# A gelu layer's forward and backward pass: a fixed order, shared half matmuls, and transposes by DMA

## The chip, the cores and the metric

The kernel runs on one core of one Trainium2 chip. A core has a matrix engine (TensorE, PE in the profile; its weight loads are PEld), a vector engine (VectorE, DVE), a scalar engine for activation functions (ScalarE, ACT), a general engine (GpSimd, POOL) and a queue engine (SyncE, SP). Operands lie in SBUF (128 partitions), matmul results in eight PSUM banks of 512 floats per partition; DMA moves data between DRAM and SBUF, within SBUF too, and can transpose 2-byte data on the way. Every engine takes its instructions in a fixed order and waits on semaphores for what other engines produce. DMAs are issued from the queues of SP, ACT and POOL.

The metric is device time of one execution in microseconds (us).

## The reference, cut to what matters

```python
B, S, D, F = 1, 2048, 448, 1792          # bf16 throughout

def fwd(x, w1, b1, w2, b2):
    h = einsum("bsd,df->bsf", x, w1) + b1
    h = gelu(h, approximate=True)         # tanh form
    return einsum("bsf,fd->bsd", h, w2) + b2

out, vjp = jax.vjp(fwd, x, w1, b1, w2, b2)
return (out, *vjp(grad_out))              # out, gx, gw1, gb1, gw2, gb2
```

So there are six large products: u = x w1, out = gelu(u + b1) w2, q = grad_out w2^T, gh = q times gelu'(u + b1), gx = gh w1^T, gw1 = x^T gh, gw2 = h^T grad_out, and the column sums gb1 and gb2. D = 448 is 3 x 128 + 64: each product over D has three full steps of 128 rows and a left-over of 64.

## The kernel before, in words

**Tiling.** F is 14 tiles of 128 ("ft"), S is 4 blocks of 512 rows ("b"), and a block is 7 pairs of ft tiles ("c"). Everything in the forward part is held transposed, F or D on the partitions: `xT_q` and `gT_q` hold a block of x and of grad_out, `w1_sb` holds w1, `w2T_sb` holds w2 transposed and halved.

**Forward part, per pair.** For each of the two ft tiles, four matmuls of 512 columns make u in a PSUM bank (L242). The fourth covers columns 320 to 447 of x; the part that the third has already counted is zeroed in the weights, and one of its rows carries b1, with a row of ones in `xT_q`. ACT reads the bank twice (gelu into `hT_blk`, L244; a square, L245), DVE reads it twice with float results (L246, L247). Then, for both tiles together (1024 elements per partition), ACT does a tanh (L248) and a square (L249), and DVE two operations (L250, L251) that give gelu' less one in `Ep`. Four more matmuls make q (L261; the overlap is zeroed in `gT_q`), and DVE multiplies `Ep + 1` by q, straight from PSUM, into `ghT_blk` (L263). POOL stores the pair's `hT_blk` and `ghT_blk` to DRAM.

**Output products.** While block b is worked on, the out and gx of block b-1 are made: per 128 rows, 14 matmuls of 448 columns (emit_M2, L191; emit_M6, L204), evicted by DVE with b2 added (L193) or by ACT (L206). SP stores them.

**Start.** Eight matmuls on zeros, then x and grad_out of block 0 and all of w2 are transposed on PE against an identity matrix that POOL makes (L100, L102, L171, L172), and copied out of PSUM by DVE and ACT. x and grad_out of blocks 1 to 3, and w1 as `w1T_sb`, are transposed by DMA from SP (L87 to L92, L272).

**Weight gradients.** These need h and gh with S on the partitions. Both are transposed by DMA from their DRAM copies: 14 transposes of 512 KB for h (L316), 14 for gh (L340). gw2 is 14 groups of 16 matmuls of 448 columns (L319); gw1 is made by column ranges of 256, 512, 512 and 512 (L377), its left-over 64 rows as half-width matmuls, two of them side by side on the two column halves of the array (L383). DVE adds up gb1 and gb2 (L311, L355 to L358), POOL reduces across partitions (L323, L363).

**Order.** Instructions are written in program order, and a scheduler places them on each engine at compile time by readiness and its own costs, so that PE's order differs from the source. Some edges are pinned by hand: transposes in a chain, plain DMAs after a batch of transposes (`pdma`), the stores of the last part after the last transpose.

Of the kernel before, what the change touches and what calls it, by code (L numbers as in the profile page):

```python
# [19 lines left out]
def kernel(  # L20
# [19 lines left out]
    assert B == 1  # L40
    NS = S // P
    NF = F // P
    KD = (D + P - 1) // P
    DL = D - (KD - 1) * P
    DOV = D - P
    assert DL == 64 and D % 16 == 0 and NF % 2 == 0
# [4 lines left out]
    SYNC_DEP = mybir.DependencyInfo(mybir.DependencyClass.Sync, mybir.DependencyReason.DATA)  # L51
    ORDER_DEP = mybir.DependencyInfo(mybir.DependencyClass.NoSync, mybir.DependencyReason.SCHED_ONLY)
# [8 lines left out]
    psum1 = ctx.enter_context(tc.tile_pool(name="psum1", bufs=3, space=bass.MemoryType.PSUM))  # L61
    psum4 = ctx.enter_context(tc.tile_pool(name="psum4", bufs=2, space=bass.MemoryType.PSUM))
    psum_acc = ctx.enter_context(tc.tile_pool(name="psum_acc", bufs=3, space=bass.MemoryType.PSUM))
    io = ctx.enter_context(tc.tile_pool(name="io", bufs=1))
    qpool = ctx.enter_context(tc.tile_pool(name="qpool", bufs=2))

    hT_dram = dram.tile([F, S], BF16, name="hT_dram")
    ghT_dram = dram.tile([F, S], BF16, name="ghT_dram")
    hT_dram_v = hT_dram.rearrange("(ft p) s -> p ft s", p=P)
    ghT_dram_v = ghT_dram.rearrange("(ft p) s -> p ft s", p=P)  # L70

    ident = const.tile([P, P], BF16, name="ident")
    make_identity(nc, ident[:])

    def chain(insts, first_after):
        prev_name = first_after
        for k, i in enumerate(insts):
            if prev_name is not None:
                tc.add_manual_dep(i.ins, prev_name, SYNC_DEP if (k == 0) else ORDER_DEP, reason="DMA transpose batch ordering")
            prev_name = i.ins.name  # L80
        return insts[-1]

    def load_quarter(q):
        rows = slice(q * SB, (q + 1) * SB)
        xq = qpool.tile([P, KD, SB], BF16, name="xT_q")
        ts = []
        ts.append(nc.sync.dma_start_transpose(out=xq[:, 0:KD - 1, :], in_=x2[rows, 0:(KD - 1) * P]))  # L87
        ts.append(nc.sync.dma_start_transpose(out=xq[:, KD - 1, :], in_=x2[rows, DOV:D]))
        nc.gpsimd.memset(xq[0:1, KD - 1, :], 1.0)
        gq = qpool.tile([P, KD, SB], BF16, name="gT_q")  # L90
        ts.append(nc.sync.dma_start_transpose(out=gq[:, 0:KD - 1, :], in_=g2[rows, 0:(KD - 1) * P]))
        ts.append(nc.sync.dma_start_transpose(out=gq[:, KD - 1, :], in_=g2[rows, DOV:D]))  # L92
        nc.gpsimd.memset(gq[0:DL, KD - 1, :], 0.0)
        return xq, gq, ts

    def pe_transpose_rows(dst, src_rows, j, on_act=False):
        ps = psum_acc.tile([P, KD, P], BF16, name="ps_acc")
        t_first = None
        for kt in range(KD - 1):
            ti = nc.tensor.transpose(ps[:, kt, :], src_rows[:, kt * P:(kt + 1) * P], ident[:])  # L100
            t_first = t_first or ti
        nc.tensor.transpose(ps[:, KD - 1, :], src_rows[:, DOV:D], ident[:])  # L102
        if on_act:
            ev_i = nc.scalar.copy(out=dst[:, :, j * P:(j + 1) * P], in_=ps[:])
        else:
            ev_i = nc.vector.tensor_copy(out=dst[:, :, j * P:(j + 1) * P], in_=ps[:])  # L106
        return t_first, ev_i

    fb = ExitStack()
    tmp = fb.enter_context(tc.tile_pool(name="tmp", bufs=3))  # L110
    blk = fb.enter_context(tc.tile_pool(name="blk", bufs=2))

    w2T_sb = const.tile([P, KD, F], BF16, name="w2T_sb")
    nc.vector.memset(w2T_sb[:, 0, 0:SB], 0.0)
    pw = psum1.tile([P, SB], F32, name="ps1")
    for i in range(8):
        nc.tensor.matmul(pw[:], lhsT=w2T_sb[:, 0, 0:P], rhs=w2T_sb[:, 0, 0:SB], start=True, stop=True)

    x_nat0 = tmp.tile([P, SPB, D], BF16, name="x_nat0", bufs=1)
    grp1 = [nc.sync.dma_start(out=x_nat0[:], in_=x2[0:SB, :].rearrange("(j p) d -> p j d", p=P))]  # L120
    w1_sb = const.tile([P, KD, F], BF16, name="w1_sb")
    nc.gpsimd.memset(w1_sb[0:DL, KD - 1, :], 0.0)

    def load_w1_cols(f0, f1, engs):
        fsl = slice(f0, f1)
        res = []
        for kt in range(KD - 1):
            res.append(engs[kt % len(engs)].dma_start(out=w1_sb[:, kt, fsl], in_=w1[kt * P:(kt + 1) * P, fsl]))
        res.append(engs[(KD - 1) % len(engs)].dma_start(out=w1_sb[DL:P, KD - 1, fsl], in_=w1[(KD - 1) * P:D, fsl]))
        return res  # L130

    def after(insts, prev_group):
        for i in insts:
            for pi_ in prev_group:
                tc.add_manual_dep(i.ins, pi_.ins.name, SYNC_DEP, reason="stagger startup loads")
        return insts

    grp1 += load_w1_cols(0, 512, [nc.scalar, nc.sync])
    grp1.append(nc.scalar.dma_start(out=w1_sb[0:1, KD - 1, :], in_=b1.rearrange("(o f) -> o f", o=1)))
    g_nat0 = tmp.tile([P, SPB, D], BF16, name="g_nat0", bufs=1)  # L140
    grp2 = [nc.sync.dma_start(out=g_nat0[:], in_=g2[0:SB, :].rearrange("(j p) d -> p j d", p=P))]
    w2_sb = const.tile([P, NF, D], BF16, name="w2_sb")
    grp1.append(nc.gpsimd.dma_start(out=w2_sb[:, 0:2, :], in_=w2[0:2 * P, :].rearrange("(ft p) d -> p ft d", p=P)))
    grp2.append(nc.gpsimd.dma_start(out=w2_sb[:, 2:NF // 2, :], in_=w2[2 * P:F // 2, :].rearrange("(ft p) d -> p ft d", p=P)))
    grp2 += load_w1_cols(512, 1024, [nc.sync, nc.gpsimd])
    after(grp2, [grp1[0], grp1[3]])
    grp3 = load_w1_cols(1024, F, [nc.gpsimd, nc.sync])
    grp3.append(nc.gpsimd.dma_start(out=w2_sb[:, NF // 2:NF, :], in_=w2[F // 2:F, :].rearrange("(ft p) d -> p ft d", p=P)))
    b2_bc = const.tile([P, D], BF16, name="b2_bc")
    grp3.append(nc.gpsimd.dma_start(out=b2_bc[:], in_=b2.rearrange("(o d) -> o d", o=1).to_broadcast((P, D))))  # L150
    after(grp3, [grp2[0], grp2[1]])

    xq0 = qpool.tile([P, KD, SB], BF16, name="xT_q")
    for j in range(SPB):
        pe_transpose_rows(xq0, x_nat0[:, j, :], j)
    nc.vector.memset(xq0[0:1, KD - 1, :], 1.0)
    gq0 = qpool.tile([P, KD, SB], BF16, name="gT_q")
    quarters = {0: (xq0, gq0)}

    def emit_gq0(pe_after, act_after):  # L160
        for j in range(SPB):
            t_first, ev_i = pe_transpose_rows(gq0, g_nat0[:, j, :], j, on_act=True)
            if j == 0:
# [21 lines left out]
    def emit_M2(b, j, hT_blk):  # L185
        if ("o", b) not in out_stage:
            out_stage[("o", b)] = io.tile([P, SPB, D], BF16, name="o_blk")
# [247 lines left out]
```

## Time and profile before

| | us |
|---|---|
| median of the 2 timed runs | 301.2 (301.1, 301.3) |
| span of the profiled execution, first to last instruction | 301.8 |
| start, until the first gh tile is done | 24.5 |
| forward part, until gw2 begins | 24.5 to 206.9 |
| gw2 and gw1 matmuls | 206.9 to 297.3 |
| end, after the last matmul | 4.5 |
| busy: PE, DVE, ACT, POOL | 284.4, 209.8, 147.6, 71.5 |

The profiled execution is not one of the timed runs; nothing of it was measured besides the span, which lies 0.6 above their median. In the page, a group line reads: line of the kernel, engine, operation, output and inputs with shapes, count, then busy time and mean duration in ns, then the idle time of the engine just before these instructions and what ended it. The chain is read as start, length, what; it goes back from the last instruction through whatever released each step. Matmuls are pipelined and their ends modelled, so the length of one (379 ns for 512 columns) is more than the distance between two.

### The profile page before, as it was taken

To read this page: it belongs to the slowest core of one execution; us is meant where nothing else is said; L and a number is where in the kernel's file an instruction comes from. 1 tells how busy PE (TensorE), PEld (TensorE's weight loads), DVE (VectorE), ACT (ScalarE), POOL (GpSimd) and SP (SyncE) were. 2 spreads that over 40 slices of the span, in tenths; PEclk is the share of its full clock that TensorE was granted. 3 is DMA by queue.
4 is the path that set the end of the run, shared out by engine and by line. 5 is a ranking of instruction groups with operands and counts; after the bars stand their busy time and mean duration, and the time that the engine had idled before them with its cause. 6 is when DMAs were issued, how large, how long until landed. Compare 5 with 4: busy or idle time off the path is not lost.

```text
span 301.8 us, 4020 instructions
## 1 busy us (share of the span) xinstructions
PE 284.4 (94%) x1520; PEld 142.5 (47%) x1520; DVE 209.8 (70%) x317; ACT 147.6 (49%) x236; POOL 71.5 (24%) x89
## 2 busy tenths in 40 slices
PE   4589799999999999999999999999999999799994
PEld 1355344444444444444444444555555558245542
DVE  0258999999999999878999778605600027857760
ACT  1099987759695756677665576112121212021211
POOL 2451010821063200522212111000210001242252
PEclk9999999999999999999999999999999999799998
DMA  4673197720579945743212314095889899999861
GB/s 134 192 206 137 41 182 168 303 114 37 130 189 375 389 155 103 213 165 130 104 72 92 116 42 187 15 223 78 169 178 171 181 213 195 183 222 164 283 206 61
DMA packets 96761, 49.18 MB, mean 163 GB/s; under 512 B 78803, under 2 KB 92596, under 8 KB 96742
## 3 DMA queue, kind: packets, MB, share of 16 engines
q1 hardware_dynamic: 91188, 31.60, 46.9%
q0 software_dynamic: 5264, 17.06, 15.0%
q10 hardware_dynamic: 290, 0.27, 0.4%
q8 instruction: 12, 0.20, 0.3%
q14 instruction: 7, 0.06, 0.1%
HBM read 7.92 MB, written 21.57 MB: 98 GB/s over the span
## 4 chain that ended last, share of the span: by engine, by line
PE 43%; DVE 9%; SPq 5%; ACT 4%; DMA 2%; issue 1%; POOL 0%; POOLq 0%; DVEq 0%
PE ps_acc L191 6%; PE ps_acc L204 6%; SPq L340 4%; DVE Ep L250 2%; DVE ghT_blk L263 2%; DVE Bt L246 2%; DMA gh_nat<-ghT_dram 2%; PE ps_2370 L377 2%; ACT Bt L249 2%; ACT Ct L248 1%; DVE Ep L251 1%; PE ps_2487 L377 1%; PE ps_2605 L377 1%; PE ps_2641 L377 1%; PE ps_2623 L377 1%
## 5 line engine op out<-in xcount | busy, mean ns | idle before, releaser
L191 PE MATMUL ps_acc<-w_sb,hT_blk 128*128 128x448 bf16 x224 | 47.7, 353 | 0.2
L204 PE MATMUL ps_acc<-w1T_sb,ghT_blk 128*128 128x448 bf16 x224 | 45.6, 353 | 0.0
L250 DVE SCALAR_TENSOR_TENSOR Ep<-Bt,A 128x1024 bf16<-128x1024 f32 x28 | 34.3, 1224 | 12.0 <-ACT Bt L249 11.7
L248 ACT ACTIVATE Ct<-Bt 128x1024 bf16<-128x1024 f32 x28 | 30.2, 1079 | 25.3 <-DVE Bt L246 25.3
L261 PEld LDWEIGHTS <-w2T_sb 128*128 128x128 bf16 x224 | 21.8, 98 | 27.5 <-issue 3.4
L242 PEld LDWEIGHTS <-w_sb 128*128 128x128 bf16 x224 | 22.1, 99 | 25.2 <-issue 2.8
L215 POOL DMA_DIRECT2D ghT_dram<-ghT_blk x28 | 20.3, 726 | 56.4 <-DVE ghT_blk L263 56.3
L355 DVE TENSOR_TENSOR gb_acc<-gh_nat 128x512 f32<-128x512 bf16 x7 | 4.8, 692 | 39.9 <-DMA gh_nat<-ghT_dram 33.1
L191 PEld LDWEIGHTS <-hT_blk 128*128 128x128 bf16 x224 | 21.8, 98 | 22.6 <-ACT hT_blk L244 0.9
L204 PEld LDWEIGHTS <-ghT_blk 128*128 128x128 bf16 x224 | 21.9, 98 | 21.2
L319 PEld LDWEIGHTS <-h_blk 128*128 128x128 bf16 x224 | 21.9, 98 | 20.5
L215 POOL DMA_DIRECT2D hT_dram<-hT_blk x28 | 20.3, 727 | 45.7 <-ACT hT_blk L244 31.3
L249 ACT ACTIVATE Bt<-Ct 128x1024 f32<-128x1024 bf16 x28 | 30.1, 1075 | 0.3
L377 PEld LDWEIGHTS <-x_all 128*128 128x128 bf16 x192 | 19.0, 100 | 21.1 <-issue 5.0
L357 DVE TENSOR_TENSOR gb_acc<-gb_acc,gh_nat 128x512 f32<-128x512 f32 x42 | 28.6, 723 | 0.3
L363 POOL PARTITION_ALL_REDUCE gb_all<-gb_acc x7 | 14.8, 2108 | 58.9 <-DVE gb_acc L358 58.9
L251 DVE TENSOR_TENSOR Ep<-Ct,Ep 128x1024 bf16<-128x1024 bf16 x28 | 19.2, 687 | 0.3
L206 ACT CAST gx_blk<-ps_acc 128x448 bf16<-128x448 f32 x16 | 8.4, 527 | 20.1 <-PE ps_acc L204 20.1
L193 DVE TENSOR_TENSOR o_blk<-ps_acc,b_bc 128x448 bf16<-128x448 f32 x16 | 9.8, 620 | 3.8 <-PE ps_acc L191 3.8
L311 DVE TENSOR_TENSOR gsum<-gsum,g_all 128x448 f32<-128x448 f32 x14 | 8.7, 625 | 0.5
L177 ACT ACTIVATE w2T_sb<-ps_acc 128x512 bf16<-128x512 bf16 x14 | 8.5, 730 | 0.0
L106 DVE COPY xT_q<-ps_acc 128x512 bf16<-128x512 bf16 x4 | 1.7, 425 | 9.7 <-PE ps_acc L102 9.7
(492 smaller groups left out, 468.7 us busy)
## 6 DMA issues: line engine op xcount, KB each, us to landing
hT_dram<-hT_blk POOLq DMA_DIRECT2D x28, 256.0 KB, 3.0
ghT_dram<-ghT_blk POOLq DMA_DIRECT2D x28, 256.0 KB, 2.7
out_dram<-o_blk SPq DMA_DIRECT2D x4, 448.0 KB
x_all<-in_x_dram SPq DMA_DIRECT2D x1, 1792.0 KB, 14.5
g_all<-in_grad_out_dram SPq DMA_DIRECT2D x1, 1792.0 KB
out_dram<-gx_blk SPq DMA_DIRECT2D x4, 448.0 KB, 3.1
out_dram<-gw_all SPq DMA_DIRECT2D x2, 784.0 KB, 5.5
out_dram<-gw_all SPq DMA_DIRECT2D x3, 384.0 KB, 2.7
```

Of the source, the lines that this page charges most:

```text
L191: nc.tensor.matmul(ps_o[:, 0:D], lhsT=hT_blk[:, ft, j * P:(j + 1) * P], rhs=w2_sb[:, ft, :], start=(ft == 0), stop=(ft == NF - 1))
L204: nc.tensor.matmul(ps_x[:, 0:D], lhsT=ghT_blk[:, ft, j * P:(j + 1) * P], rhs=w1T_sb[:, ft, :], start=(ft == 0), stop=(ft == NF - 1))
L215: i = eng.dma_start(out=out, in_=in_)
L242: mm_i = nc.tensor.matmul(ps1[:], lhsT=w1_sb[:, kt, fcols], rhs=xq[:, kt, :], start=(kt == 0), stop=(kt == KD - 1))
L248: tanh_i = nc.scalar.activation(out=Ct[:], in_=Bt[:], func=ACT.Tanh, scale=1.0 / 3.0)
L249: nc.scalar.activation(out=Bt[:], in_=Ct[:], func=ACT.Square)
L250: nc.vector.scalar_tensor_tensor(out=Ep[:], in0=Bt[:], scalar=1.0, in1=A[:], op0=ALU.subtract, op1=ALU.mult)
L251: nc.vector.tensor_tensor(out=Ep[:], in0=Ct[:], in1=Ep[:], op=ALU.subtract)
L261: nc.tensor.matmul(ps4[:], lhsT=w2T_sb[:, kt, fcols], rhs=gq[:, kt, :], start=(kt == 0), stop=(kt == KD - 1))
L319: nc.tensor.matmul(ps_w[:, 0:D], lhsT=h_blk[:, st, :], rhs=g_all[:, st, :], start=(st == 0), stop=(st == NS - 1))
L357: nc.vector.tensor_tensor(out=acc[:], in0=acc[:], in1=gh_nat[:, 2 * k:2 * k + 2, :], op=ALU.add)
L377: nc.tensor.matmul(ps_w[:, 0:wpair], lhsT=x_all[:, st, kt * P:(kt + 1) * P], rhs=gh_pair[:, st, :], start=(st == 0), stop=(st == NS - 1))
```

## The change

The forward part is written anew, in a fixed order on every engine (no scheduler), in 28 steps i, one per pair, over all blocks.

- **Two steps ahead.** Step i makes u and h of pair f = i + 2 (`LEAD = 2`, starting at i = -2) and q and gh of pair i.
- **Left-over halves side by side.** The 64 left-over rows of u sit in partitions 64 to 127 (`wt1`), those of q in partitions 0 to 63 (`w2T_t`). Each is a matmul over 64 rows, and the two are issued in turn, to the two row halves of the array and to different PSUM banks. b1 is no longer a row of the product: it is turned to a column on PE once and added by ACT.
- **Elementwise work.** ACT writes u + b1 as bf16 into SBUF (`U`), and gelu, the square and tanh work from there on 1024 elements; DVE uses bf16 operations with one input and an immediate, or with two inputs, and only the product with q still reads PSUM.
- **Transposes.** x and grad_out of block 0 and all of w2 come by DMA transpose. gh goes from SBUF to SBUF by DMA transpose (`turn_gh`, three per block) into `gh_nat` and is not stored to DRAM; h still goes through DRAM.
- **Output products** are filled in after each step: up to 4 pairs of matmuls in steps before 14, up to 8 from then on, the rest after step 27. At most four outputs are open at a time; each is stored by POOL as soon as it is evicted.
- **Weight gradients.** gw1 comes first, then gw2; ACT evicts each group and issues its store itself. The sums for gb1 and gb2 are interleaved on DVE.
- PSUM has two pools of four banks: u, q and gw2 share one; the outputs and gw1 the other.

The core of the diff (removed lines of the old forward part are left out):

```diff
+    sched = ctx.enter_context(tc.manual_schedule())
...
+    def pe_tails(f, k):
+        if k is not None:
+            PQ[k] = [psq.tile([P, SB], F32, name="pq", tag="pq") for _ in range(2)]
+        for a in range(2):
+            if f is not None:
...
+                nc.tensor.matmul(PU[f][a][:], lhsT=wt1[DL:P, fc], rhs=xT[b][DL:P, KF, :], start=False, stop=True,
+                                 tile_position=(DL, 0), skip_group_check=True)
+            if k is not None:
...
+                nc.tensor.matmul(PQ[k][a][:], lhsT=w2T_t[0:DL, fc], rhs=gT[b][0:DL, KF, :], start=True, stop=False,
+                                 tile_position=(0, 0), skip_group_check=True)
...
+    def act_forward(f):
...
+            nc.scalar.activation(out=U[f][:, a, :], in_=PU[f][a][:], func=ACT.Identity, bias=b1T[:, ft:ft + 1])
+        nc.scalar.activation(out=hT[b][:, 2 * p:2 * p + 2, :], in_=U[f][:], func=ACT.Gelu_apprx_tanh)
+        nc.gpsimd.dma_start(out=hT_dram_v[:, 2 * p:2 * p + 2, b * SB:(b + 1) * SB], in_=hT[b][:, 2 * p:2 * p + 2, :])
+    def act_square(k):
+        nc.scalar.activation(out=A[k][:], in_=U[k][:], func=ACT.Square, scale=math.sqrt(3.0 * GELU_A * GELU_C))
+    def dve_cubic(k):
+        nc.vector.tensor_scalar(out=Z[k][:], in0=A[k][:], scalar1=3.0 * GELU_C, scalar2=None, op0=ALU.add)
+        nc.vector.tensor_tensor(out=Z[k][:], in0=Z[k][:], in1=U[k][:], op=ALU.mult)
+    def act_tanh(k):
+        nc.scalar.activation(out=Z[k][:], in_=Z[k][:], func=ACT.Tanh, scale=-1.0 / 3.0)
+    def dve_gate(k):
+        nc.vector.tensor_scalar(out=a_[:], in0=a_[:], scalar1=GELU_C, scalar2=None, op0=ALU.add)
+        nc.vector.tensor_tensor(out=a_[:], in0=a_[:], in1=hT[b][:, 2 * p:2 * p + 2, :], op=ALU.mult)
+        nc.vector.tensor_scalar(out=a_[:], in0=a_[:], scalar1=-0.5, scalar2=None, op0=ALU.add)
+        nc.vector.tensor_scalar(out=z_[:], in0=z_[:], scalar1=1.0, scalar2=None, op0=ALU.add)
+        nc.vector.tensor_tensor(out=z_[:], in0=z_[:], in1=a_[:], op=ALU.mult)
+    def dve_gh(k):
+            nc.vector.scalar_tensor_tensor(out=ghT[b][:, 2 * p + a, :], in0=Z[k][:, a, :], scalar=1.0, in1=PQ[k][a][:],
+                                           op0=ALU.add, op1=ALU.mult)
+    def turn_gh(b, p0, p1):
+        nc.sync.dma_start_transpose(out=gh_nat[:, b, 2 * p0:2 * p1, :, :].rearrange("p ft j f -> p (ft j) f"),
+                                    in_=ghT[b][:, 2 * p0:2 * p1, :].rearrange("p ft s -> p (ft s)"))
...
+    for i in range(-LEAD, NSTEP):
+        f = i + LEAD
+        fok, kok = f < NSTEP, i >= 0
+        if fok:
+            pe_u_fulls(f)
+        if fok or kok:
+            pe_tails(f if fok else None, i if kok else None)
+        if kok:
+            pe_q_fulls(i)
+            act_tanh(i)
+        if fok:
+            act_forward(f)
+        if 0 <= i + 2 < NSTEP:
+            act_square(i + 2)
+        if 0 <= i + 1 < NSTEP:
+            dve_cubic(i + 1)
+        if kok:
+            dve_gate(i)
+            dve_gh(i)
+        evictions()
...
+        fill(4 if i < 2 * NPAIR else 8, last_f(i) - 1, i - 1)
+    while open_units or todo or finished:
+        fill(28, NSTEP, NSTEP)
+        evictions()
+    x_nat = blk.tile([P, NS, D], BF16, name="x_nat", tag="hT")
+    nc.sync.dma_start(out=x_nat[:], in_=x2.rearrange("(st p) d -> p st d", p=P))
...
+    for ft in range(4):
+        load_h(ft)
...
+    for ft0, n in ((0, 4), (4, 4), (8, 4), (12, 2)):
+        for kt in range(KF):
+            gw1_full(ft0, n, kt)
+            emit_sum(3)
+        if ft0 == 4:
+            gw1_tail(0, 4)
+        if ft0 == 12:
+            gw1_tail(8, 3)
+    for ft in range(NF):
+        gw2_tile(ft, 2 if ft == NF - 1 else 1)
+        if ft + 4 < NF:
+            load_h(ft + 4)
+        emit_sum(3)
```

`pe_u_fulls` and `pe_q_fulls` issue the three full k-steps of u and q for both tiles of a pair (six matmuls each). The line numbers that the prediction gives for the changed kernel are those of its file: L148 forward full matmuls, L158 and L163 the tails, L173 backward full matmuls, L200 and L202 one-input operations of `dve_gate`.

More of the change, by code (lines that the diff above doesn't have):

```diff
@@ L96, in pe_transpose_rows @@
[L96 to L107, printed above, removed]
@@ L121 @@
[L121 to L136, printed above, removed]
```

524 lines of the change are left out of this document (236 added, 288 removed).

## The prediction

> **What bounds the kernel now.** I read the page's slices first, then a table of stretches, then the chain and the groups. All times are us unless marked ns. The slices: 40 of 7.5 each, busy tenths per engine, and the clock granted to TensorE.
>
> ```profile
> PE   4589799999999999999999999999999999799994
> DVE  0258999999999999878999778605600027857760
> ACT  1099987759695756677665576112121212021211
> PEclk9999999999999999999999999999999999799998
> ```
>
> PE is full from the sixth slice to the thirty-fifth. Since a busy PE may be a modelled one, I check it by spacing, with the chain (start, length, what):
>
> ```profile
> 148.30 0.86 PE ps_1435 L261 x4
> 196.31 10.59 PE ps_acc L204 x56
> 206.90 3.03 PE ps_1977 L319 x16
> ...
> 252.85 5.59 DMA gh_nat<-ghT_dram
> 258.44 0.14 issue
> 258.57 5.30 PE ps_2370 L377 x16
> 263.87 3.45 PE ps_2388 L377 x16
> 267.32 3.45 PE ps_2406 L377 x16
> 270.78 1.87 PE ps_2424 L383 x32
> 272.64 3.56 PE ps_2487 L377 x16
> ```
>
> A matmul of 512 columns costs 0.86/4 = 0.2155, one of 448 columns 10.59/56 = 0.189 (3.03/16 the same). Of the half-width pairs of L383, which run side by side, 16 pairs of 256 columns take 1.87, 0.117 a pair; the first group after them takes 3.56 instead of 3.45, so a return from the split array costs 0.11. From 24.5 to 207 TensorE issues at these spacings almost without a gap, so the forward part is bound by the number of matmuls. At 252.85 it waits for gh, then runs a group at 5.30: 1.85 above its neighbours. The vector side has these prices (groups: busy, mean ns | idle before):
>
> ```profile
> L250 DVE SCALAR_TENSOR_TENSOR Ep<-Bt,A 128x1024 bf16<-128x1024 f32 x28 | 34.3, 1224 | 12.0 <-ACT Bt L249 11.7
> L251 DVE TENSOR_TENSOR Ep<-Ct,Ep 128x1024 bf16<-128x1024 bf16 x28 | 19.2, 687 | 0.3
> L358 DVE TENSOR_TENSOR gb_acc<-gb_acc 128x256 f32<-128x256 f32 x7 | 2.9, 420 | 0.0
> L248 ACT ACTIVATE Ct<-Bt 128x1024 bf16<-128x1024 f32 x28 | 30.2, 1079 | 25.3 <-DVE Bt L246 25.3
> L215 POOL DMA_DIRECT2D hT_dram<-hT_blk x28 | 20.3, 727 | 45.7 <-ACT hT_blk L244 31.3 <-DMA w1T_sb<-in_w_dram 7.7 <-issue 6.7
> ```
>
> 1024 float elements cost 1.224, 1024 bf16 ones 0.687, 256 float ones 0.420.
>
> **The change, part by part.**
>
> *TensorE work.* The fourth k-step of each product was a full 512-column matmul for 64 useful rows; 56 + 56 of them become 56 pairs, a saving of 56 x 0.2155 = 12.1. If a pair shares its time as those of L383 do, a pair costs 0.2155, plus a switch in and out of the split array at each step, 2 x 0.1 by the 0.11 above. The 56 transposes of w2 and the 32 of x and g leave PE; their cost lies in the start, below.
>
> *A step.* PE issues 6 forward full matmuls (1.29), the tails in two slots (0.43), 6 backward full ones (1.29), the switches (0.2), and a fill for the output products: 8 matmuls of 448 (1.51) in steps -1 to 13, 16 (3.02) in steps 14 to 26. That is 4.7 early and 6.24 late.
>
> *DVE.* Each step has two reads of PSUM as L263 (two take 1.28 in the chain), three two-input bf16 operations as L251 (0.69 each, 2.07), and four one-input bf16 operations, a kind that no row shows. Their bounds: 0.27, the 256-column memset of L114, and 1.22, L250. I take 0.42, the row of 256 steps (L358): two inputs of bf16 already go two elements per step in L251, and one input leaves half the reading free. If it were L251's rate it is 0.69. Less 0.18, since two of the four depend on nothing just before them and such neighbours start 0.60 apart instead of 0.69, a step is 1.28 + 2.07 + 1.68 - 0.18 = 4.85; with queue gaps 4.9. The Trainium skill's "VectorE: DVE Perf Modes" (The perf-mode tier table) lists 693 ns for such an operation on 2048 elements; by it half the length is estimated at 0.43 and the sum moves by under 1; no run here shows it.
>
> So early steps are bound by DVE (4.9 against 4.7) and late ones by PE (6.24, against 4.9 plus an output eviction of 0.62 in about 12 of 14 steps, 5.4).
>
> *ACT.* Two reads of PSUM (0.60 + 0.50 as L244; the per-row bias is between nothing and 0.13 more, as L177's 0.73 shows) and three of 1.08 make 4.3 to 4.6, plus 0.53 for a gx copy in some steps: hidden behind DVE, uncovered from 4.9 on.
>
> *Waits.* The backward tail of step i waits until DVE has emptied step i-1's bank (four banks, two per product). Behind it on PE stand the second forward tail, the backward matmuls and the fill. The forward side is two steps ahead, so ACT still has what it needs: tanh of i+1 needs only DVE's first 1.1 of step i. I cost this at nothing beyond the DVE bound. When four output groups finish together (step 6), DVE evicts all four before its next step: 4 x 0.62 = 2.5, on the path.
>
> *SP and POOL.* gh is no longer stored and reloaded; SP issues three transposes per block from SBUF to SBUF, a kind not in the trace. Nearest row: L340's from DRAM, 512 KB, 2.1 to 2.5 each on SP and 5.3 to landing. Lower bound 1.2, the smaller transposes of L88; upper 5.3, if SP were held until the data has landed. I take 2.4 for the 512 KB ones: some 9 of a block's 35 to 44. A dozen us each would be needed before the next block's loads, queued behind on SP, come late. The last one delays only x_nat and g_nat, which have 14.5 to land (row of x_all) while 112 output matmuls run 21; beyond that every us counts. POOL loses 28 stores of gh (0.73 each) and gains 32 of the outputs instead of 8 on SP; two per step, 1.5, hidden.
>
> *Start.* Now the first backward eviction ends at 24.5. After: the b1 transpose heads PE's queue and needs ident, which POOL had ready at 10.1 after 7.4 of idle; I keep 9.9. The second w1 slice is issued by POOL only after ident (about 1.0 + 0.9 + 0.6) and lands 3.7 later, near 15.5. After that idle PE runs 8 matmuls at half clock, as at 12.56 before (1.86 per 4): 3.4. Then ACT 1.1 + 3 x 1.08 and DVE 1.1 + 2.6 + 1.3 follow, partly overlapped: 26. x and g of block 0 and the first w2 quarter are six transposes of 1.25 to 1.65 on SP, issued by 9 and landed by 14; the rest of w2 (1.3 MB) by 24 at the rate of w1T (1.6 MB, 10.2 to landing), needed from 33 by step 2. Bounds: 23 if nothing waits for POOL's loads, 36 if w1T has to land first.
>
> *Weight gradients.* 144 matmuls of 512 (31.0), 48 of 256 (5.2), 32 half-width pairs (16 x 0.2155 + 16 x 0.1625 = 6.05) and 224 of 448 (42.4): 84.7, against 90.4 from 206.90 to 297.33 now. The wait at 252.85 goes: gh is in SBUF already, and the h transposes, one per 3.03 of PE, have four buffers, 9 of cover against 4.7 to land. The gh operand is now read in runs of 256 bytes. L377 reads one run of 1024 at full rate, L383 runs of 512 at 0.117 instead of 0.109 a pair: between nothing and 7% of 42.3, 3. I take nothing, since L383's excess is also what a split array could cost; it cannot gain, the spacing being one column per clock.
>
> *Sum*, against the profiled span: 26 for step 0; 13 steps of 4.9 and the 2.5: 92.2; rest of step 14, 4.95; 11 steps of 6.24, 68.6; steps 26 and 27 without forward work, 4.95 + 3.44; the 112 left over, 21.2: 195.3 (206.9 now). Plus 84.7: 280.0. The end after the last matmul, 4.5 as now (297.33 to 301.8): 284.5. The timed median is 0.6 below the span: **284**.
>
> **Rivals.**
>
> *Tails not side by side* (the change would not do what it says). For: no row shows two halves of the rows. Against: two halves of the columns do share in L383. Late steps +0.43 x 13, early ones 5.1 against 4.9, +3: 293.
>
> *Start starved.* All loads are now on SP's transposes; before, DMA share in the first 24.5 was 0.63 with less to move. If block 0 waits until w1T has landed (10.2 after 20): +10, 294.
>
> *DVE becomes the bound throughout; the slower side.* With e more per step the cost is 13e early and 14(e - 0.8) late. Equal to now at e = 1.05, slower by 2% from 1.26. At L251's 0.69 for the one-input operations e is 1.07: 302. If DVE is held up while POOL issues its two DMAs per step (2 x 0.727, 52 in 28 steps, 1.36): 25, so 309. Against: L251 ran 680 to 693 ns all through, while POOL issued. At L250's 1.22, e is 3.2: 359. The Trainium skill's "SBUF — State Buffer" (Who interferes with whom) says that a one-input operation in a two-port mode and POOL's descriptor writing lock each other out of one port pair. By that rule one or the other stands still; no run here shows it.
>
> **Chances.** Forecast 0.60 (277 to 291), tails 0.08, start 0.08, DVE at 302 0.06, DVE at 309 0.12, at 359 0.03, others 0.03. What a measurement tells from no change is 2%, 295.2 to 307.2. Faster: 0.60, the larger part of the tails case: 0.65. Within: the rest of it, the start's late half, 302: 0.17. Slower: 0.18. The range goes from 275 (one-input operations at 0.27, start as now) to 310, leaving out 359 and the unknown.
>
> **What would show it.** L200 and L202 near 0.42 and steps of 4.9 on DVE before about 92, 6.2 on PE after; L158 and L163 starting within 0.1 of each other; gw starting near 195 with x_nat landed; no PE idle over 1 in gw. Wrong if one-input operations take 0.69, if DVE has gaps while POOL issues, or if PE waits for a transpose.

## The result, and the profile after

The changed kernel takes 311.3 us (310.7 and 311.9) against 301.2: 1.034 times the time before, 95% interval 1.025 to 1.042. It is **slower**; 284 was forecast, in a range of 275 to 310. The profiled execution has a span of 310.1 and is one of the two timed runs (311.9). So against the predicted span of 284.5 there are 25.6 to explain.

The slices of the changed kernel (40 of 7.75 each; busy tenths per engine, and the clock granted to TensorE):

```profile
PE   7301994969699999999999999999999999999995
DVE  0000296896999999998888898720399999000000
PEclk9655897988999999999999999999999999999999
```

From the twelfth slice on the picture is the forecast one: TensorE (PE) is full to the end, there is no hole where gw1 starts, and VectorE (DVE) is nearly full in the early steps. All the trouble is in the first ten slices. PE is nearly empty in slices 3 and 4, and in slices 2 to 4 its clock is granted at 0.5 to 0.6. The chain (start, length, what) says what the first 68 us hang on:

```profile
9.21 12.47 SPq L107
21.72 11.35 SPq L108
33.12 29.14 SPq L128
62.30 5.61 DMA xT<-in_x_dram
67.96 2.56 PE pu L148 x6
...
123.24 1.29 PE pu L148 x6
...
129.50 1.29 PE pu L148 x6
...
200.51 10.59 PE ps_o L230 x56
211.11 10.59 PE ps_x L230 x56
221.70 20.72 PE ps_w L369 x96
...
264.42 42.53 PE ps_v L393 x240
```

The chain begins on SP's queue, with the first transpose at 0.73, and stays there until block 1's x has landed at 67.9: the second transposes of w2 (L107, L108) hold SP for 12.47 and 11.35, the transpose of w1 (L128) for 29.14. In the kernel before, the same transpose of w1, same instruction and shape, held it for 6.54:

```profile
41.60 6.54 SPq L272 DMA_TRANSPOSE w1T_sb<-in_w_dram  x1
```

Behind that, the late steps follow each other at 123.24, 129.50: 6.26. The 112 left-over matmuls take 21.2 (200.51 to 221.70), and the weight gradients run from 221.70 to 306.95: 85.2. These are the forecast numbers. What PE waited for in the first 125 us (engine, line, releaser: us in total, times, longest):

```profile
PE pu L148 <- DMA w_f<-in_w_dram: 18.0, 1, 18.0
PE pq L163 <- DMA w2T_t<-in_w_dram: 4.2, 1, 4.2
PE ps_x L230 <- DVE st L238: 2.4, 1, 2.4
PE pu L148 <- DMA xT<-in_x_dram: 2.3, 1, 2.3
```

The largest wait is not for a transpose: it is for the second slice of w1, a plain load of 192 KB that POOL issued at 10.1 and that took 19.9 to land. The first slice, which ACT issued at 0.7 together with SP's first transpose, took 2.8. And the price of the elementwise work (groups: busy, mean ns | idle before):

```profile
L183 POOL DMA_DIRECT2D hT_dram<-hT x28 | 20.2, 720 | 117.0 <-ACT hT L182 116.6
...
L191 DVE TENSOR_SCALAR Z<-A 128x1024 bf16<-128x1024 bf16 x28 | 11.9, 425 | 34.4 <-ACT A L187 33.1
```

A one-input bf16 operation on 1024 elements takes 0.425, and POOL's DMA issue still takes 0.72.

**What the DMA engines did.** SP's transposes run on the queue called q1 in the profile, POOL's plain loads on q0, ACT's on q10. The stretch from 41 to 53 of the kernel before, when the transpose of w1 and a little of x and grad_out were alone (queue: packets, MB, share of 16 engines):

```profile
q1 hardware_dynamic: 7698, 1.95, 79.6%
```

The stretch from 33 to 48 of the changed kernel, transposes beside POOL's queue, which then carried plain loads and the first stores of h:

```profile
DMA packets 1682, 1.81 MB, mean 121 GB/s; under 512 B 1346, under 2 KB 1354, under 8 KB 1682
...
q1 hardware_dynamic: 1275, 0.32, 71.8%
q0 software_dynamic: 407, 1.50, 48.3%
```

For the first stretch, 7698 packets took 0.796 x 16 x 12 us, so 20 ns each by the profile's packet times, and 164 GB/s were moved; but the stretch ends with over 3 us in which hardly anything is in flight, and from 44.9 to 49.7, with the transpose of w1 by itself, it was 283 GB/s. Side by side, a transposed packet took 0.718 x 16 x 15 us / 1275 = 135 ns, and both kinds together moved only 121 GB/s. (Packet times overlap: the two shares add up to 120%.) This is more than taking turns: 1275 packets of 20 ns on 16 engines are 1.6 us, and 1.50 MB at the some 280 GB/s that a stretch of mostly loads reaches in a run below are 5.4; together 7, where 15 passed. From 18 to 33, with loads alone on POOL's queue, a transposed packet took 0.713 x 16 x 15 us / 1864 = 92 ns, at 124 GB/s.

### The profile page after: what moved, and what is told of

It reads as the page before. It is cut to its first block, busy times and chain, and to the rows that moved or that the text cites. A ratio compares the mean times of both kernels' runs of the same rounds, so it can differ in the third digit from the quotient of the medians.

```text
span 310.1 us, 3733 instructions
## 1 busy us (share of the span) xinstructions
PE 274.9 (89%) x1392; PEld 126.0 (41%) x1406; DVE 188.1 (61%) x300; ACT 142.0 (46%) x187; POOL 63.9 (21%) x84
## 4 chain that ended last, share of the span: by engine, by line
PE 63%; SPq 20%; DVE 11%; ACT 2%; DMA 2%; issue 1%; DVEq 0%
PE ps_v L393 14%; PE ps_w L369 12%; PE ps_x L230 11%; PE ps_o L230 10%; SPq L128 9%; PE pq L173 6%; PE pu L148 6%; SPq L107 4%; SPq L108 4%; DVE ghT L209 3%; PE pu L158 2%; PE ps_w L380 2%; DMA xT<-in_x_dram 2%; DVE Z L204 2%; DVE A L201 2%; DVE Z L192 2%
## 5 line engine op out<-in xcount | busy, mean ns | idle before, releaser
L181 ACT ACTIVATE U<-pu,b1T 128x512 bf16<-128x512 f32 x56 | 35.5, 683 | 66.2 <-PE pu L158 66.1
L148 PE MATMUL pu<-xT,w_f 128*128 128x512 bf16 x161 | 43.3, 399 | 20.6 <-DMA w_f<-in_w_dram 18.0
L230 PE MATMUL ps_x<-w1T_sb,ghT 128*128 128x448 bf16 x224 | 45.0, 352 | 2.4 <-DVE st L238 2.4
L230 PE MATMUL ps_o<-w_sb,hT 128*128 128x448 bf16 x224 | 45.2, 354 | 0.1
L393 PE MATMUL ps_v<-g_nat,h_nat 128*128 128x448 bf16 (+1 forms) x240 | 42.6, 340 | 0.0
L173 PE MATMUL pq<-gT,w2T_f 128*128 128x512 bf16 x161 | 41.2, 389 | 0.8 <-issue 0.7
L209 DVE SCALAR_TENSOR_TENSOR ghT<-Z,pq 128x512 bf16<-128x512 bf16 x56 | 36.5, 684 | 8.4 <-PE pq L173 6.5
L369 PE MATMUL ps_w<-gh_nat,x_nat 128*128 128x512 bf16 (+1 forms) x192 | 36.7, 353 | 0.0
L148 PEld LDWEIGHTS <-w_f 128*128 128x128 bf16 x168 | 16.6, 100 | 42.8 <-DMA w_f<-in_w_dram 18.9
L230 PEld LDWEIGHTS <-hT 128*128 128x128 bf16 x224 | 22.0, 98 | 22.3 <-issue 1.6
L357 DVE TENSOR_TENSOR acc<-acc,gh_nat 128x1792 f32<-128x1792 f32 x14 | 30.0, 2142 | 0.5
L182 ACT ACTIVATE hT<-U 128x1024 bf16<-128x1024 bf16 x28 | 29.6, 1057 | 0.9
L187 ACT ACTIVATE A<-U 128x1024 bf16<-128x1024 bf16 x28 | 29.1, 1039 | 0.0
L173 PEld LDWEIGHTS <-w2T_f 128*128 128x128 bf16 x168 | 14.4, 99 | 28.1 <-issue 15.4
L163 PE MATMUL pq<-gT,w2T_t 64*128 64x512 bf16 x56 | 18.4, 396 | 4.7 <-DMA w2T_t<-in_w_dram 4.2
```

The lines of the kernel that those rows point to most:

```text
L148: nc.tensor.matmul(PU[f][a][:], lhsT=w1_f[:, kt, fc], rhs=xT[b][:, kt, :], start=(kt == 0), stop=False, skip_group_check=True)
L173: nc.tensor.matmul(PQ[k][a][:], lhsT=w2T_f[:, kt, fc], rhs=gT[b][:, kt, :], start=False, stop=(kt == KF - 1), skip_group_check=True)
L181: nc.scalar.activation(out=U[f][:, a, :], in_=PU[f][a][:], func=ACT.Identity, bias=b1T[:, ft:ft + 1])
L182: nc.scalar.activation(out=hT[b][:, 2 * p:2 * p + 2, :], in_=U[f][:], func=ACT.Gelu_apprx_tanh)
L187: nc.scalar.activation(out=A[k][:], in_=U[k][:], func=ACT.Square, scale=math.sqrt(3.0 * GELU_A * GELU_C))
L209: nc.vector.scalar_tensor_tensor(out=ghT[b][:, 2 * p + a, :], in0=Z[k][:, a, :], scalar=1.0, in1=PQ[k][a][:], op0=ALU.add, op1=ALU.mult)
```

## The experiments

Theories at the start. **Mixing**: transposes and plain loads in flight together slow each other. **Volume**: there are simply too many transposed bytes on one queue. **Order**: block 1's x stands behind w1T on SP. **Late issue**: POOL's loads are late, because they stand behind the identity matrix, or because a queue whose descriptors POOL writes is the weak one. The runs of this part were executed once each, except the start in turns and the one queue, each with and without more fill, which have four executions; so small differences in time are read from the traces or not at all.

### The same transfers, kept apart

```diff
+        i1 = eng.dma_start(out=w1_f...)        # in load_w1, load_w2: remember the plain loads
+        plain.extend([i1, i2])
...
         i0 = nc.sync.dma_start_transpose(out=w2T_f[:, :, f0:f1], in_=w2[f0:f1, DL:D])
+        if f0 > 0:
+            for pl in plain:
+                tc.add_manual_dep(i0.ins, pl.ins.name, HOLD, ...)
```

> The same transfers in the same order on every queue, but SP's transposes of the rest of w2 (L107, second call), and with them w1T and all behind it, wait until the plain loads of w1 and w2 have landed. MIXING theory (transposes and plain loads in flight together slow each other): the plain loads, 3.2 MB from 9 on, run at the 306 GB/s that plain loads alone showed before and have landed by 21 to 23; the second w1 slice is there by 14 to 17 instead of 30.0, the first gh tile near 27 instead of 41.8; the rest of w2 (1.3 MB) takes SP 5 to 8 instead of 23.8, w1T 6.5 to 10 instead of 29.1; step 13's gh near 97 to 100 instead of 118.4, in all 288 to 293. VOLUME theory (too many transposed bytes on one queue, whoever is beside them): rest of w2 21 to 45, w1T to 74, both only shifted; block 0 waits at step 2 until about 47 and block 1's x until about 79: 311 to 325. ORDER theory (what costs is that block 1's x stands behind w1T on SP): no better than the changed kernel, 311 or more.

Measured: 295.1, span 293.3 against 310.1 for the changed kernel. SP's part of its timeline (start, us, what):

```profile
25.46 5.24 SPq L111 DMA_TRANSPOSE w2T_f<-in_w_dram  x1
30.75 1.41 SPq L115 DMA_TRANSPOSE w2T_t<-in_w_dram  x1
32.20 6.74 SPq L135 DMA_TRANSPOSE w1T_sb<-in_w_dram  x1
```

The same three transposes hold SP for 5.24, 1.41 and 6.74 instead of 12.47, 11.35 and 29.14, with the same bytes on the same queue: volume falls. So does order as the main cause, since block 1's x still stands behind w1T here. The plain loads landed in 3.1 to 9.2 instead of 15 to 22.8, the last at about 25 (21 to 23 expected). The first gh tile was done at 25.6 instead of 41.8. Two us above the expected range: the held transposes came too late for step 2, where PE waited 5.0 for w2T_t. The 306 GB/s in the expectation were a poor yardstick, since that stretch of the kernel before moved stores, not loads.

### Only the order on SP

```diff
+    load_x(1)
+    load_g(1)
     nc.sync.dma_start_transpose(out=w1T_sb[:], in_=w1[:, :])
```

> Only the order on SP: x and grad_out of block 1 are issued ahead of w1T. ORDER theory: the wait for block 1's x (2.3, and PE's slow restart after it, about 1) goes and w1T still lands before its first use near 77: 306 to 308. MIXING theory: the wait for block 1's x goes, but the waits for the second w1 slice (18.0) and for w2T_t (4.2) stay as they are, and w1T lands some 6 later, near 75: 306 to 310. VOLUME theory: as MIXING. What it tells apart: whether the order on SP carries more than 5 of the 26.

Measured: 305.0, a little below both ranges; the wait for block 1's x is gone, and the one for w2T_t too. But the run is no clean price of the order: its first gh tile was done at 38.9 instead of 41.8, and SP issued the second w2T_f in 5.98 instead of 12.47, although nothing ahead of them differs. While both kinds are in flight, the durations vary by several us from one execution to the next. What can be read: the order carries a few us at most of the 25.6. And w1T, issued here at 48.47, when the loads had landed, held SP for 7.30: the same transpose for the third time, fast as soon as no load is beside it.

### The plain loads on ACT's queue

```diff
-    load_w2(nc.gpsimd, 0, 2)
+    load_w2(nc.scalar, 0, 2)
...                                        # all loads of w1, w2 and b2 alike
```

> The plain loads of w1, w2 and b2 go from POOL's queue, where the first stands behind the identity matrix and is issued at 9.05, to ACT's queue, from 0.7 on; nothing is held. LATE-ISSUE theory (POOL issues too late, or its software-written queue is what is slow beside transposes): the loads land by about 15, the first gh tile comes near 26 and w2T and w1T run at the rates of before (1.6 MB in 10): 287 to 293. MIXING theory: the second w1 slice comes earlier, since it now stands 5 to 9 earlier beside fewer transposes, but the rest of w2 and w1T stay as slow while plain loads run: the wait for w2T_t moves to 45 to 51 and grows by what the first one lost: 300 to 310.

Measured: 304.2, inside the range of mixing. But not for the expected reason: the loads landed in 3.9 to 10.1, the second w1 slice came in time, and from 9 to 22 both kinds together moved 229 GB/s. What was late is ACT itself (its timeline):

```profile
12.65 1.04 ACTq L100 DMA_DIRECT2D w_f<-in_w_dram  x1
25.82 0.47 ACTq L101 DMA_DIRECT2D wt<-in_w_dram  x1
...
27.04 1.26 ACT L181 ACTIVATE U<-pu,b1T 128x512 bf16<-128x512 f32 x2 [19.45 <-issue]
```

ACT stood for 12 us in front of its thirteenth DMA and evicted its first u at 27.04 instead of 11.68. SP's second w2T_f was issued at 11.50 and landed 14.3 later, at 25.8: the profile puts ACT's wait down to this transpose. That the DMA needed a completion semaphore which the transpose still held fits the times, but is not shown. The time of this run says nothing on the queue; the next one issues fewer DMAs on ACT.

### ACT's queue with fewer DMAs

```diff
-    load_w2(nc.gpsimd, 0, 2)               # and all other loads on POOL
+    load_w2(nc.scalar, 0, NF)
+    load_w1(nc.scalar, 256, F)             # five DMAs on ACT in all; b1 goes to POOL
```

> The changed kernel with the plain loads of w1 and w2 on ACT's hardware queue from 0.7 on, in five DMAs, few enough that none waits for a transpose; nothing is held, so the rest of w2 and w1T are transposed beside them. SOFTWARE-QUEUE theory (only loads whose descriptors POOL writes are starved beside transposes): the two together move some 230 GB/s, as in the run with all loads on ACT; w1 and w2 land by 18, the rest of w2 by 30, first gh tile near 24: 285 to 290. ANY-QUEUE theory (mixing costs whatever queue the plain loads are on): the rest of w2 lands at 40 or later, in all 295 to 306.

Measured: 300.7, in the any-queue range. But its sign, the rest of w2 at 40 or later, did not come: that had landed by 35, and from 2 to 16 the two kinds together moved 247 GB/s, above the 230 of the software-queue theory. The time was lost to things that the edit brought in: the identity matrix is ready only at 13.2, and the second w1 slice, now part of one large load, lands at 22.3; PE waited 6.3 and 5.3 for them, and for no transpose. ACT's fifth DMA still stood 5.3 before it was issued. The kernel before took 305.4 beside this run and the two on halves and lead below, and 301.2 to 301.6 beside the others, so a few us are not to be read from its time.

On the queue the traces say this much. From 2 to 16 a transposed packet kept its 20 to 33 ns, but the transposes got few turns: grad_out's two held SP for 11.3 instead of 2.9. From 18 to 22 it took 101 to 116 ns, at 73 to 131 GB/s in all, but by then b2's load and a store of h were on POOL's queue too (23 packets), so this stretch does not tell the queues apart. The run with all loads on ACT does: from 9 to 18, with nothing on POOL's queue, a transposed packet took 0.49 x 16 x 9 us / 3704 = 19 ns at 250 GB/s, and from 18 to 24, still with nothing there, 0.835 x 16 x 6 us / 1848 = 43 ns at 168 GB/s. So transposes can be slowed beside ACT's loads too, but less than beside POOL's (92 ns at 124 GB/s). That POOL's queue is the weak one, the second half of late issue, is therefore not refuted; it is likely from these rates, not shown.

### The second w1 slice on ACT: with the hold, and without

Both move one slice; the first has the hold on top, so their difference is the hold alone.

```diff
     load_w1(nc.scalar, 0, 256)
+    load_w1(nc.scalar, 256, 512)
...
-    load_w1(nc.gpsimd, 256, 512)
```

> As the run that holds w2's rest and w1T behind the plain loads, and the second w1 slice is issued by ACT right after the first, from about 1.8. MIXING theory: the second slice lands before 10 and no longer delays PE; the first gh tile near 23 to 25, the rest as in the run without this: 285 to 291, 2 to 4 below that run. VOLUME theory: the first gh tile as early, but step 2 waits until about 47 and block 1 until about 79 all the same: 311 to 325.

> The changed kernel with one edit: the second w1 slice is issued by ACT right after the first, so PE's wait of 18.0 for it goes; nothing is held. LATE-SLICE theory (the 18.0 for that slice, not the transfers beside it, is the loss): first gh tile near 24 and everything behind it 18 earlier: 291 to 294. MIXING theory: plain loads and transposes still share the time from 10 to 50, so the wait moves to w2T_t at step 2 (landing at 45 or later instead of 33) and to block 1's x: 302 to 309, and the difference to the run that has the hold as well (291.7) is the price of mixing by itself.

Measured: 291.7 with the hold and 312.5 without, spans 289.9 and 310.7. Mixing costs **20.8 us** here, with the same transfers on the same queues. This is one execution of each; without the early slice the hold was worth 16.2 (311.3 to 295.1). Without the hold, SP's timeline and PE's longest wait:

```profile
9.90 15.36 SPq L107 DMA_TRANSPOSE w2T_f<-in_w_dram  x1
25.31 14.33 SPq L108 DMA_TRANSPOSE w2T_t<-in_w_dram  x1
39.69 13.80 SPq L128 DMA_TRANSPOSE w1T_sb<-in_w_dram  x1
```

```profile
PE pu L148 <- DMA w_f<-in_w_dram: 22.1, 1, 22.1
```

With the hold:

```profile
22.98 4.27 SPq L111 DMA_TRANSPOSE w2T_f<-in_w_dram  x1
27.30 2.44 SPq L115 DMA_TRANSPOSE w2T_t<-in_w_dram  x1
29.78 6.79 SPq L135 DMA_TRANSPOSE w1T_sb<-in_w_dram  x1
```

The late-slice theory falls: giving PE the slice that it had waited 18.0 for only moved the wait to the next slice, and made it 22.1. From 14 to 46 this run moved 121 GB/s, and from 10 to 23 the held one moved 279. Nor does the hold merely let the loads that PE needs go first: with it the plain loads have landed by 23 instead of 45, and w1T has left SP at 36.6 instead of 53.5, so both kinds are done sooner. It was expected 302 to 309 and came out above, since I had put the wait at w2T_t and not at a plain load again.

### The halves on the same rows

```diff
-        nc.sync.dma_start_transpose(out=gT..., in_=g2[rows, DL:D])   # and w2T_f alike
+        nc.sync.dma_start_transpose(out=gT..., in_=g2[rows, 0:KF * P])
...
-lhsT=w2T_t[0:DL, fc], rhs=gT[b][0:DL, KF, :], ... tile_position=(0, 0)
+lhsT=w2T_t[DL:P, fc], rhs=gT[b][DL:P, KF, :], ... tile_position=(DL, 0)
```

> The run with the held transposes and the early second slice, with one edit: both left-over halves lie in partitions 64 to 127 (w2 and grad_out are cut at 384 instead of at 64), so that the two tails share one row half and cannot run side by side. If side by side is worth what the changed kernel's trace shows (0.22 per pair less than two matmuls, against two switches of 0.1): PE per step +0.43, or +0.23 if the switches stay; early steps are hidden behind DVE's 5.24, the some 13 bound by PE are not: 294 to 298 against 291.7. If the halves bring nothing, 291 to 292; if every step pays 0.43, 303.

Measured: 300.2, span 298.5 against 289.9 with the halves apart. The tails start one after the other, every 0.22, while in the kernel with the halves apart the two of a pair start together. First this run, then that one:

```profile
148.33 0.39 PE L165 MATMUL pu<-xT,wt 64*128 64x512 bf16 x1
148.55 0.38 PE L170 MATMUL pq<-gT,w2T_t 64*128 64x512 bf16 x1
148.77 0.38 PE L165 MATMUL pu<-xT,wt 64*128 64x512 bf16 x1
148.98 0.38 PE L170 MATMUL pq<-gT,w2T_t 64*128 64x512 bf16 x1
149.29 1.47 PE L180 MATMUL pq<-gT,w2T_f 128*128 128x512 bf16 x6
```

```profile
148.20 0.39 PE L165 MATMUL pu<-xT,wt 64*128 64x512 bf16 x1
148.20 0.39 PE L170 MATMUL pq<-gT,w2T_t 64*128 64x512 bf16 x1
148.43 0.38 PE L165 MATMUL pu<-xT,wt 64*128 64x512 bf16 x1
148.43 0.38 PE L170 MATMUL pq<-gT,w2T_t 64*128 64x512 bf16 x1
148.74 1.47 PE L180 MATMUL pq<-gT,w2T_f 128*128 128x512 bf16 x6
```

From the last tail to the next full matmul it is 0.31 in both, so the switch of 0.09 stays and the whole 0.43 per step is the price: late steps are 6.69 apart instead of 6.26. The run is 8.6 us longer in span, more than I expected of it (294 to 298). Of this 2.0 are there by the gh of step 13, 1.3 of them at the first gh tile already, and 6.1 come from there to step 26, where 13 steps pay 0.43 (5.6). The prediction's rival had priced the whole at 9 (293 against 284), but partly in the wrong place: early steps stay at DVE's 5.23 in both runs, so its 3 for them did not come, and the start made up for it. What the shared array is shown to be worth is the 6 in the late steps.

### One step of lead instead of two

```diff
-    LEAD = 2
+    LEAD = 1
...
-        if 0 <= i + 2 < NSTEP:
-            act_square(i + 2)
+        if 0 <= i + 1 < NSTEP:
+            act_square(i + 1)
```

> The run with the held transposes and the early second slice, with LEAD = 1 (and the square one pair ahead instead of two). LEAD theory (the distance of two is what keeps DVE and PE apart): each step becomes the chain u tail, ACT 1.28 + 1.06 + 1.04, DVE 1.1 + 2.7 + 1.3, some 9 instead of 5.24 in 28 steps, less the fill that no longer has to run afterwards: 370 to 400. If the lead doesn't matter (PE or DVE throughput bounds either way): 292 to 298.

Measured: 333.2, span 331.5. The lead matters, at 42 us, but less than expected: most early steps are 6.6 to 6.9 apart and the late ones 7.4 to 7.6, not 9, and the fourfold eviction makes one of 15.1. The edit also takes away one of three buffers of `U`, whose number follows `LEAD`, so the price is that of both. I had added up a chain in which nothing overlaps; the forward tail of the next pair does not wait for the gh of this one. The waits of the two engines in this run:

```profile
PE pq L170 <- ACT U L188: 24.0, 26, 3.7
...
DVE Z L198 <- ACT A L194: 64.1, 28, 7.9
```

Each engine waits for ACT once in nearly every step. With two steps of lead the row of PE is absent, and that of DVE is 14.2 in 10 waits.

### A start in turns

```diff
+    turn1 = load_w2(nc.gpsimd, 0, 4) + load_w1(nc.gpsimd, 512, 1280) + load_w2(nc.gpsimd, 4, 8)
+    turn2 = hold(load_w2T(512, 1280), turn1)
+    turn3 = hold(load_w1(nc.gpsimd, 1280, F) + load_w2(nc.gpsimd, 8, NF), turn2)
+    turn3.append(...b2...)
+    hold(load_w2T(1280, F), turn3)
+    load_x(1)
+    load_g(1)
     nc.sync.dma_start_transpose(out=w1T_sb[:], in_=w1[:, :])
...                                        # two w1 slices on ACT; b1's turn on PE behind the first u
```

> The changed kernel with a start in turns, each held until the one before has landed: transposes of x, grad_out and the first w2 rows beside the two first w1 slices (ACT); then plain w2 to row 1024 and w1 to column 1280; then the transposes of w2's rows 512 to 1280; then the rest of w1, w2 and b2; then the rest of w2's transposes, block 1's x and grad_out, w1T. b1's turn on PE comes behind the first u. If the turns keep both kinds at the rates that they have alone, no wait of PE for a DMA is left after step 0: 4.5 less than the run with one hold, and 2 for b1: 284 to 288. If waiting for a turn costs more than mixing (2 to 3 per turn, three turns, on the path of step 2): 290 to 293.

Then the same with more fill in steps 6 to 13:

```diff
-        fill(4 if i < 2 * NPAIR else 8, last_f(i) - 1, i - 1)
+        fill(4 if i < NPAIR - 1 else 6 if i < 2 * NPAIR else 8, last_f(i) - 1, i - 1)
```

> The run with the start in turns, and the fill of output products raised from 4 to 6 pairs of matmuls in steps 6 to 13, where DVE's step of 5.24 leaves PE 0.5 idle. If PE's idle time there is free, 16 pairs of 0.378 move into it, 6.0 less behind step 27, of which 8 x 0.26 come back as steps of 5.5: 4 less than the run without, 280 to 284. If DVE's evictions of the outputs that then finish earlier take it back: no difference.

Measured: 288.3 for the start in turns, 0.955 of the time before (0.951 to 0.958), and **286.8** with the fill, 0.948 (0.943 to 0.953). Both beat both kernels; the first ends at the upper edge of its range, the second 3 above its own. The slices of PE and DVE in the start in turns:

```profile
PE   8499999499999999999999999999999999999995
DVE  0169999959999999986788986202999995000000
```

PE's hole at the start is gone. The other hole, in the eighth slice, is a wait of 4.2 for DVE to evict four outputs that finish together. The fill brought 1.6 of the expected 4. The matmuls did move: 88 instead of 120 are left behind the last q, 6.0 less. But the last q comes 4.3 later instead of the 2.1 put for it: 2.0 by step 13, of which 0.9 at the fourfold eviction, and 2.3 behind it, since without the extra fill PE starts the forward matmuls of step 14 2.1 before the gh of step 13 is done, and with it 0.7 after. More would not have helped by itself: x_nat, which gw1 needs, lands at 196.7 in this run, just as the last left-over matmul ends.

### All start-up loads in SP's queue

```diff
-    turn1 = load_w2(nc.gpsimd, 0, 4) + ...  # all holds go
+    load_w2(nc.sync, 0, 4)
+    load_w1(nc.sync, 512, 1280)
+    load_w2(nc.sync, 4, 8)
+    load_w2T(512, 1280)
...                                        # the same order as the turns; b2 stays on POOL
```

> The start in turns, without the holds: the plain loads of w1 and w2 stand in SP's queue between the transposes, in the same order as the turns, and only the queue's order keeps the two kinds apart (b2 alone stays on POOL). MIXING theory, if one queue works its entries off nearly one after the other: the loads start at about 10 as with POOL, nobody waits for a landing, and PE's wait of 2.8 for the first output operand goes: 285 to 288, against 288.3 with the holds. If entries of one queue run together as those of two do: the mixing is back, rest of w2 and w1T crawl, 298 to 312.

> The run with all start-up loads in SP's queue, and 6 instead of 4 pairs of output matmuls in steps 6 to 13. With the holds this brought 1.6 (286.8 against 288.3, where 4 was expected, since DVE's evictions took part of it back). Expected 1 to 3 below the run without: 283 to 287; 297 or more if the one queue mixes.

Measured: 291.8, 0.966 (0.961 to 0.971), and 288.5 with the fill, 0.958 (0.955 to 0.961). The first lies 4 above its range and the second 1.5, both far below those for mixing: the order of one queue keeps the kinds nearly apart without any hold. It is not better than the holds, since the loads now stand behind six transposes and the transposes behind them: PE waits 5.2 for the first w2 slice (3.0 with the holds and the fill), and SP was held 8.53 by the first w2T_f behind the loads (2.40 with the holds), so the kinds still overlap at their borders.

## Why the prediction was wrong

**The step that failed is the start**, in the words of the prediction: x and g of block 0 and the first w2 quarter "are six transposes of 1.25 to 1.65 on SP, issued by 9 and landed by 14; the rest of w2 (1.3 MB) by 24 at the rate of w1T (1.6 MB, 10.2 to landing)". The first half held: the six took 1.26 to 1.62 each and were issued by 9.2. The second half did not: the rate of w1T came from a stretch in which w1T was alone, and the kernel before keeps it alone by hand (`pdma`, the chain). One of the prediction's own lines shows it: L215, POOL's store of h, was idle for 7.7 until w1T had landed. In the changed kernel this edge is gone, and the transposes stand beside 3.2 MB of plain loads. The rest of w2 landed at 51, w1T held SP until 62.3, and POOL's second w1 slice, put at "3.7 later, near 15.5", came at 30. The prediction's own sign of being wrong, "if PE waits for a transpose", came too, at 4.2 and 2.3.

By the terms of the sum: the first gh tile at 41.8 instead of 26 is 15.8. Two more waits for a transpose (4.2 and 2.3), with PE's slower clock behind them, stretch steps 2 to 6 by 6.3 beyond DVE's step. That step is 5.23 instead of 4.9, which over 13 is 4.3; the fourfold eviction was 0.2 to 0.3 cheaper than put. Together 26.2 at the gh of step 13 (118.4 against 92.2). From there to the last matmul 188.6 passed (103.3 and 85.2), where 187.8 were forecast. The end is 1.4 shorter, and that makes the 25.6. With the start in turns the span is 286.6, 2.1 above the forecast; there the first gh tile is done at 21.3, 4.7 earlier than forecast, and the 13 steps take 73.8 instead of 66.2.

**The rival "start starved" named the right place, with a price that was too small and a mechanism that did not occur.** It let block 0 wait until w1T had landed 10.2 after its issue, for 10; it kept the rate of a transpose that is alone. What block 0 waited for was a plain load of w1, behind the same traffic. The slowing itself was in no case of mine, and 294 still came out faster than before. The bound "36 if w1T has to land first" fell short in the same way: 41.8. That the measured 311 lies near the rival of 309 is luck; its reason accounts for half a us (below).

The Trainium skill's "DMA: Bandwidth & Descriptors" (Rules for kernel authors) says that a transpose next to ordinary DMAs needs nothing. It says so in a row on outputs that come out corrupt, and no run here speaks against that; it must not be read as a rule on time, since the hold alone is worth 16 to 21 here. The same page (Queues, rings and completion order) says that a DMA engine takes the queues in turn, a packet at a time. That agrees with a stretch of the run with five loads on ACT's queue: from 8 to 16 it shows 1271 transposed packets and 1265 plain ones, if a packet of the profile is one of the page's, which nothing here shows. Turns of one packet are unequal: 253 bytes a transposed one, 3.7 KB a plain one in the changed kernel (1.95 MB / 7698 and 1.50 MB / 407). It does not account for the total, which fell to 121 GB/s.

**The right steps.** *One-input operations*: 0.425, 0.42 was put; the estimate from the Trainium skill's "VectorE: DVE Perf Modes" (The perf-mode tier table), 0.43, agrees. *Tails side by side*: yes, 0.22 a pair and 0.2 of switches a step; the run with the halves on the same rows prices this at 6 in the late steps. *Late steps*: 6.26 (6.24). *DVE step*: the mechanism right, the size off: 5.23 (4.9). The step that begins at 97.28 shows where: its operations are busy for 5.05 (5.03 by the terms), four of them start 0.03 to 0.04 after the end of the one before, and 0.11 passes on either side of the PSUM product. These gaps are 0.35 in all, where 0.05 was put for them. *gh within SBUF*: landing 5.7 in the median, x_nat in time, no wait of PE in gw. *gw*: 85.2 (84.7). *POOL's DMA issue against DVE*: POOL took 0.720 per issue (0.727 before). Of DVE's 112 one-input operations 38 overlap an issue of POOL; four of these took 0.03 to 0.24 longer than usual (L203 at 110.34 took 0.66 instead of 0.42), and no other did. So the lock-out that the Trainium skill's "SBUF — State Buffer" (Who interferes with whom) describes is seen here, but for 0.5 us in all and not for 1.36 per step.

**What stays open.** Why transposes and loads slow each other beyond taking turns, and how much of it is POOL's queue. A busy DVE that keeps POOL from writing descriptors does not account for it: from 10 to 23 of the changed kernel DVE was busy for 1.1 of 13 us, and 127 GB/s were moved. Stores do not do it to the same degree: from 63 to 85 of the changed kernel transposed packets took 0.858 x 16 x 22 us / 12069 = 25 ns beside 1.11 MB on POOL's queue, which by then carried only stores. But these were also fewer bytes at a time, so whether it is their kind or their number isn't settled.

## What to carry to other kernels

A DMA's rate read from a profile holds for what was in flight beside it; before putting it into a sum, look at what the source keeps away from it, above all at edges written by hand, and ask whether the change keeps them. A rewrite that removes ordering edges should be priced with the queues running against each other, both kinds of traffic slowed; shown here is transposes on SP against loads on POOL's queue. And when a wait for one operand is cut away at a starved start, look for the next operand on the same queues: the wait moved, and grew from 18.0 to 22.1.

## What the runs showed of the hardware

- Transposes on SP beside plain loads on POOL's queue: 124 GB/s in all and 92 ns a transposed packet with loads alone (18 to 33), 121 and 135 with some stores among them (33 to 48), against 283 GB/s and 20 ns for the transpose of w1 alone and 279 GB/s for a stretch of mostly loads. Beside loads on ACT's queue it was 19 to 43 ns at 168 to 250 GB/s. The same w1 transpose held SP for 29.1, 13.8, 7.3, 6.7 and 6.5 in different company.
- The slowing is not steady: with nothing changed ahead of it, the same transpose of w2 took 5.98 in one run and 12.47 in another.
- Matmuls on the two row halves share their time fully (0.22 a pair), and leaving the split array costs 0.09, also when all halves were on the same rows.
- A DMA issue on ACT stood for 12 us until a transpose of another queue had landed, and ACT's arithmetic behind it.
- An issue of POOL lengthened a one-input bf16 operation of DVE by up to 0.24, in 4 of the 38 that overlapped one.
